# Linear attention and expert layer on one core: token loads cast by the DMA, scores and products on parts of the TensorE array, one activation recipe in two variants

## The chip, the cores and the metric

The kernel runs on one core of one Trainium2 chip. The metric is device time in microseconds (us), the median of several executions. "Batch" below means one of the eight batches of the problem; the kernel works on them one after another, and attention of batch b+1 runs while the expert layer of batch b does.

## The reference, cut to what matters

Eight batches, 8 heads, 576 tokens, 64 numbers a head. 32 packed queries p attend to the tokens; then the tokens attend to the 32 packed results; the result, as a row of 512 numbers, goes through two weight matrices with a piecewise activation between them.

```python
def sm_attn(qq, kk, vv):              # softmax(scale * q k^T) v
    ...
p_packed = sm_attn(p, k, v)           # 32 x 64 for each batch and head
out = sm_attn(q, p_packed, p_packed)  # 576 x 64 for each batch and head
x = out.transpose(0, 2, 1, 3).reshape(4608, 512)
h = x @ w_in                          # 512 -> 2048
g = where(h >= 1, h, where(h <= -1, 0, (h + 1)**2 / 4))
y = g @ w_out                         # 2048 -> 512
```

Both kernels use that x @ w_in = A @ M, where A holds the attention weights of the tokens over the packed rows and M is (packed result) @ (w_in), 32 rows for each head. So the expert layer's first product takes A and M, and x is never made.

## The kernel before

Only the parts that the change touches. Tokens are loaded in f32 and cast to bf16 on three engines; the remainder of 64 tokens (576 = 4 x 128 + 64) has its own load and casts.

```python
psA = ... bufs=2 (PSUM)   # all of attention
psH = ... bufs=2 (PSUM)   # hidden tiles h
psO = ... bufs=2 (PSUM)   # output tiles o

def load_tokens(src, b, tag, eng):
    t = stg.tile([P, H, NC4, D], f32, ...)      # 4 x 128 tokens
    eng.dma_start(...)
    r = stg.tile([REM, H, D], f32, ...)         # 64 tokens
    eng.dma_start(...)
# ... cut: cast_steps: two casts of 128x1024 and two of 64x256 for each of k, v, q;
#          batches 0 and 1 on VectorE, ScalarE and GpSimd, later ones on GpSimd

def scores(c0, n):
    for c in range(n):
        for hp in range(HP):          # 2 heads at once, p in a block-diagonal, half zeros
            nc.tensor.matmul(sp[:, c, hp], kT[:, hp, ...128 tokens], pT_blk[:, b, hp], ...)
    nc.scalar.activation(ex, sp, AF.Exp, scale=scale)
# ... cut: packed() (5 matmuls of 320 columns for 4 heads, masked), packed_t() (transposes)

def mk(g, f):                          # M, 4 heads x 512 columns of w_in
    for j in range(2):                 # the other half of ppT's rows is zero
        nc.tensor.matmul(mp, ppT[:, g, j], w_in_sb[:, 2 * g + j, f * FW:(f + 1) * FW], ...)
    ...                                # copied to SBUF by ScalarE or VectorE

def hidden_tile(b, fi):
    h = psH.tile([P, 2, FW], f32, tag="h")
    # ... cut: four matmuls of 288 columns, h = A, M
    nc.scalar.activation(r, hv, AF.Relu, bias=half, scale=0.5)        # r = relu(h/2 + 1/2)
    if (fi * PB_SHARE) % 8 < PB_SHARE:
        nc.gpsimd.tensor_mul(u, r, r)                                 # 10 of 16 tiles
    else:
        nc.scalar.activation(u, r, AF.Square)                         # 6 of 16
    nc.vector.scalar_tensor_tensor(dst, u, 1.0, hv, ALU.min, ALU.max) # max(min(r*r, 1), h)
```

The last line: the third engine in the row reads `hv`, the PSUM tile, again. So the tile is held until VectorE is done.

The softmax here doesn't subtract the row's maximum and nothing guards it: scores larger than these inputs give would overflow.

Of the kernel before, what the change touches and what calls it, by code (L numbers as in the profile page):

```python
# [11 lines left out]
def kernel(  # L12
# [20 lines left out]
    P = 128  # L33
# [4 lines left out]
    HP = H // 2  # L38
    G = H // 4
    NC4 = 4  # L40
    REM = S - NC4 * P
    HALF = S // 2
    KF = d_ff // P
    FW = 512
    PB_SHARE = 5
# [5 lines left out]
    stg = ctx.enter_context(tc.tile_pool(name="stg", bufs=1))  # L51
# [5 lines left out]
    psA = ctx.enter_context(tc.tile_pool(name="psA", bufs=2, space=bass.MemoryType.PSUM))  # L57
    psH = ctx.enter_context(tc.tile_pool(name="psH", bufs=2, space=bass.MemoryType.PSUM))
    psO = ctx.enter_context(tc.tile_pool(name="psO", bufs=2, space=bass.MemoryType.PSUM))



    def load_tokens(src, b, tag, eng):
        t = stg.tile([P, H, NC4, D], f32, tag=tag, name=tag)
        eng.dma_start(
            t.rearrange("p h c d -> p h (c d)"),
            src[b, :, :NC4 * P, :].rearrange("h (p c) d -> p h (c d)", c=NC4))
        r = stg.tile([REM, H, D], f32, tag=tag + "r", name=tag + "r")
        eng.dma_start(r, src[b, :, NC4 * P:, :].rearrange("h p d -> p h d"))
        raw[(tag, b)] = (t, r)  # L70

    def load_all(b, eng):
        for n, t in (("k", k), ("v", v), ("q", q)):
            load_tokens(t, b, n, eng)

    raw = {}
    load_all(0, nc.sync)


    p_nat = const.tile([P, B, G, D], bf16)  # L80
    p_v = p.rearrange("b (g h) n d -> (h n) b g d", g=G)
    nc.gpsimd.dma_start(p_nat[:, :1], p_v[:, :1])

    w_in_sb = const.tile([P, HP, d_ff], bf16)
    w_out_sb = const.tile([P, KF, d_model], bf16)
    w_in_v = moe_w_in.rearrange("(c p) f -> p c f", p=P)
    w_out_v = moe_w_out.rearrange("(c p) f -> p c f", p=P)

    def load_w_in(f):
        nc.gpsimd.dma_start(w_in_sb[:, :, f * FW:(f + 1) * FW], w_in_v[:, :, f * FW:(f + 1) * FW])  # L90
# [5 lines left out]
    mask = const.tile([P, 4, D], bf16)  # L96
    nc.vector.memset(mask, 0.0)
    for i in range(4):
        nc.vector.memset(onesblk[i * NP:(i + 1) * NP, i * NP:(i + 1) * NP], 1.0)
        nc.vector.memset(mask[i * NP:(i + 1) * NP, i], 1.0)  # L100
    half = const.tile([P, 1], f32)
    nc.vector.memset(half, 0.5)


    VB = H * D + D
    kb, qb, vb = [], [], []
    for i in range(2):
        for lst, nm in ((kb, "kb"), (qb, "qb")):
            t = const.tile([P, NC4 + 1, H * D], bf16, name=f"{nm}{i}")
            nc.vector.memset(t[REM:, NC4], 0.0)  # L110
            lst.append(t)
        t = const.tile([P, NC4 + 1, VB], bf16, name=f"vb{i}")
        nc.vector.memset(t[REM:, NC4], 0.0)
        nc.vector.memset(t[:, :NC4, 4 * D:5 * D], 1.0)
        nc.vector.memset(t[:REM, NC4, 4 * D:5 * D], 1.0)
        vb.append(t)

    def cast_steps(nm, b, engs):

        t, r = raw.pop((nm, b))  # L120
        d = {"k": kb, "q": qb, "v": vb}[nm][b % 2]

        def cp(e, dst, src):
            if e is nc.scalar:
                e.copy(dst, src)
            else:
                e.tensor_copy(dst, src)  # L127

        st = []
        for g in range(G):  # L130
            o = g * 5 * D if nm == "v" else g * 4 * D
            st.append(lambda o=o, g=g: cp(engs[g], d[:, :NC4, o:o + 4 * D].rearrange("p c (h d) -> p h c d", h=4),
                                          t[:, 4 * g:4 * g + 4]))
        for g in range(G):
            o = g * 5 * D if nm == "v" else g * 4 * D
            st.append(lambda o=o, g=g: cp(engs[2], d[:REM, NC4, o:o + 4 * D].rearrange("p (h d) -> p h d", h=4),
                                          r[:, 4 * g:4 * g + 4]))
        return st


    pT_blk = const.tile([P, B, HP, 2, NP], bf16)
    nc.vector.memset(pT_blk, 0.0)

    def build_pT(b0, b1):
        n = b1 - b0
        tp = psA.tile([P, n, 4, NP], bf16, tag="a", name="tpp")
        for b in range(b0, b1):
            nc.tensor.transpose(tp[:, b - b0].rearrange("p h n -> p (h n)"),
                                p_nat[:, b].rearrange("p g d -> p (g d)"), ident)

        for g in range(G):
            for h2 in range(2):
                nc.vector.tensor_copy(pT_blk[h2 * D:(h2 + 1) * D, b0:b1, 2 * g:2 * g + 2, h2, :],  # L153
                                      tp[g * D:(g + 1) * D, :, h2::2, :])
# [3 lines left out]
    def transposes(src, tag, base, rbase, width):  # L158

        T = tr.tile([P, HP, width], bf16, tag=tag, name=tag, bufs=1 if tag == "kT" else 2)  # L160

        def pair(c0):
            tp = psA.tile([P, HP, 2, P], bf16, tag="a", name="tp")
            for hp in range(HP):
                for c in range(2):
                    nc.tensor.transpose(tp[:, hp, c], src[:, c0 + c, hp * P:(hp + 1) * P], ident)  # L166
            nc.vector.tensor_copy(T[:, :, base + c0 * P:base + (c0 + 2) * P],  # L167
                                  tp.rearrange("p h c t -> p h (c t)"))

        def rest():  # L170
            n = P if width > S else REM
            tp = psA.tile([P, HP, P], bf16, tag="a", name="tp")
            for hp in range(HP):
                nc.tensor.transpose(tp[:, hp], src[:, NC4, hp * P:(hp + 1) * P], ident)
            nc.vector.tensor_copy(T[:, :, rbase:rbase + n], tp[:, :, :n])

        return T, [lambda: pair(0), lambda: pair(2), rest]

    def attention(b, split=False):

        st = []
        kT, sk = transposes(kb[b % 2], "kT", 0, NC4 * P, S + REM)

        base, rbase = (0, NC4 * P) if b % 2 == 0 else (REM, 0)
        qT, sq = transposes(qb[b % 2], "qT", base, rbase, S)
        vt = vb[b % 2]
        ex = att.tile([P, NC4 + 1, H * NP], bf16, tag="ex")

        def scores(c0, n):
            sp = psA.tile([P, n, HP, 2 * NP], f32, tag="a", name="sp")  # L190
            for c in range(n):
                for hp in range(HP):
                    nc.tensor.matmul(sp[:, c, hp], kT[:, hp, (c0 + c) * P:(c0 + c + 1) * P],  # L193
                                     pT_blk[:, b, hp].rearrange("p h n -> p (h n)"), start=True, stop=True)
            nc.scalar.activation(ex[:, c0:c0 + n].rearrange("p c n -> p (c n)"),  # L195
                                 sp.rearrange("p c a n -> p (c a n)"), AF.Exp, scale=scale)

        st += sk[:2] + [lambda: scores(0, 2), sk[2], lambda: scores(2, 2)]
        st += ([lambda: scores(4, 1)] + sq) if split else (sq[:1] + [lambda: scores(4, 1)] + sq[1:])

        ppT = att.tile([P, G, 2, P], bf16, tag="ppT")

        def packed(g):

            pp = psA.tile([P, 5 * D], f32, tag="a", name="pp")
            for c in range(NC4 + 1):
                nc.tensor.matmul(pp, ex[:, c, g * P:(g + 1) * P], vt[:, c, 4 * g * D:(4 * g + 5) * D],  # L207
                                 start=(c == 0), stop=(c == NC4))
            one, val = (4 * D, 0) if g == 0 else (0, D)
            rs = att.tile([P, 1], f32, tag="rs", name="rs")  # L210
            nc.vector.reciprocal(rs, pp[:, one:one + 1])
            pb = att.tile([P, 4 * D], bf16, tag="pb", name="pb")
            nc.vector.scalar_tensor_tensor(pb, pp[:, val:val + 4 * D], rs,
                                           mask.rearrange("p h d -> p (h d)"), ALU.mult, ALU.mult)
            return pb

        def packed_t(g, pb):
            tp = psA.tile([P, 2, P], bf16, tag="a", name="ppt")
            for j in range(2):
                nc.tensor.transpose(tp[:, j], pb[:, j * P:(j + 1) * P], ident)  # L220
            nc.vector.tensor_copy(ppT[:, g], tp)

        box = {}

        def put(key, fn):
            box[key] = fn()

        for g in range(G):
            st.append(lambda g=g: put(g, lambda: packed(g)))
        for g in range(G):  # L230
            st.append(lambda g=g: packed_t(g, box[g]))


        M = att.tile([P, G, d_ff], bf16, tag="M")
        A = att.tile([P, G, S], bf16, tag="A")
        M_of[b], A_of[b] = M, A

# [31 lines left out]
        if split:  # L269
            return st + pr + nm, ms  # L270
# [165 lines left out]
```

## Time and profile before

| | before |
|---|---|
| median | 334.59 us (three runs, 333.87 to 337.23; 334.45 with a fourth, taken beside the kernel after) |
| profiled span | 334.0 us |
| TensorE busy | 282.1 us, 84% |
| ScalarE, VectorE, GpSimd busy | 62%, 54%, 49% |

The page of the kernel before. The first two lines are the busy time of each engine, with its share of the span and the number of instructions. Each digit of the two rows is one of 40 equal slices: the busy share of TensorE in tenths, and the TensorE clock that was granted in tenths of full speed. Then the shares of the chain of work that ended last, and three groups of instructions: what they write and read, shapes, count | busy us, mean ns of one | idle time just before them and what ended most of it.

```profile
span 334.0 us, 5198 instructions
PE 282.1 (84%) x1879; PEld 164.9 (49%) x1912; DVE 180.3 (54%) x324; ACT 206.7 (62%) x371; POOL 162.2 (49%) x190
...
PE   0274868887878998999899999999999999988894
...
PEclk9998599997999999999999999999999999999999
...
PE 34%; issue 17%; POOL 16%; DMA 11%; DVE 10%; ACT 10%; POOLq 0%; SPq 0%; ACTq 0%
...
L298 POOL TENSOR_TENSOR u<-r 128x576 f32<-128x576 f32 x80 | 91.7, 1148 | 126.8 <-ACT r L295 117.7
L301 DVE SCALAR_TENSOR_TENSOR hT<-u,h 128x576 bf16<-128x576 f32 x128 | 96.2, 752 | 94.7 <-POOL u L298 80.3
...
L295 ACT ACTIVATE r<-h,half 128x576 f32<-128x576 f32 x128 | 94.7, 741 | 69.7 <-PE h L288 67.0
```

TensorE is busy 84% of the time, but its row shows that this is two different things: 90% and more from about the twentieth slice on, and mostly 70 to 80% at first. (The clock row prints 9 where the trace has no clock record, here before 26.7 us. The transposes at 7.65 us came 107 ns apart, and those at 50 us 56 ns, so TensorE was at half speed at first.) The chain gives TensorE only 34%; the hidden tile's three steps (ScalarE r, GpSimd u, VectorE hT) and "issue" share much of the rest. These steps take 741, 1148 and 752 ns. In the last batch a tile holds its PSUM buffer for 3.34 us on average, from its first matmul to the end of hT; with two buffers that allows a tile every 1.67 us, and they came 1.75 us apart.

To see the stages apart, the hidden tile's last write (hT; 128 of them, 16 a batch) helps. In the trace of the kernel before, the 17th hT, the first of batch 1, ends at 84.52 us, the 113th, the first of batch 7, at 289.24 and the last at 315.45. The first hT of batch 3 ends at 151.99.

Windows of all engines, kernel before: batches 1 to 6, and batches 3 to 6 alone. Columns: window, its length, busy time (and count) of TensorE, its weight loads, VectorE, ScalarE and GpSimd, granted clock, DMA share, GB/s.

```profile
84.52:289.24 204.72, 191.65 (x1321) 114.67 (x1346) 125.10 (x213) 146.57 (x270) 104.98 (x115) 1.00 0.37 105
151.99:289.24 137.25, 131.26 (x914) 78.81 (x930) 84.31 (x144) 99.29 (x183) 61.04 (x64) 1.00 0.19 61
```

So: start 84.5 us; six batches in 204.7 us, 34.1 us each (34.3 in batches 3 to 6); last batch and tail 44.8 us. In the last stretch the hidden tiles take 26.2 us and the tail 18.5.

The timeline of TensorE in the middle, kernel before (start, length, engine, line, what it writes and reads, count). The lengths overlap, because the ends are modelled; the cost of a group is the distance from its start to the next one's.

```profile
189.60 0.28 PE L193 MATMUL sp<-pT_blk,kT 128*128 128x64 bf16 x4
189.72 1.24 PE L321 MATMUL o<-w_out_sb,hT 128*128 128x512 bf16 x5
...
195.77 0.84 PE L207 MATMUL pp<-vb_133,ex 128*128 128x320 bf16 x5
196.45 0.28 PE L220 MATMUL ppt<-ident,pb 128*128 128x128 bf16 x2
...
207.07 0.59 PE L259 MATMUL mp<-w_in_sb,ppT 128*128 128x512 bf16 x2
207.50 0.29 PE L249 MATMUL sm<-eT,onesblk 128*128 128x288 bf16 x1
```

Four score matmuls take 0.12 us, five packed ones 0.68, two for M 0.43. Counted so, a batch's M (16 matmuls) costs 3.44 us and all of its attention 9.27 us. The expert layer's own o and h take 23.4 us. Together TensorE needs 32.7 us a batch; the batch takes 34.1. The middle is mostly TensorE's, with about 1.4 us of stalls a batch.

Where the stalls come from is in the waits of TensorE between 85.5 and 289.5 us, kernel before (engine, what it wanted to do, what it waited for: us in total, times, longest):

```profile
PE h L288 <- DVE hT L301: 9.2, 13, 2.1
PE mp L259 <- DVE M L264: 2.3, 5, 0.5
```

A hidden tile waits for the PSUM that an earlier one still holds: 9.2 us over six batches, 1.5 us a batch.

### The profile page before, as it was taken

How to read it: one execution, taken by the hardware profiler on the slowest of the kernel's cores; microseconds unless marked ns; L12 is line 12 of the kernel's file. 1: busy time of each engine (PE TensorE's matmuls, PEld its weight loads, DVE VectorE, ACT ScalarE, POOL GpSimd, SP SyncE). 2: the span in 40 equal slices, each digit the busy share in tenths (PEclk: the TensorE clock that was granted, in tenths of full speed). 3: DMA queues.
4: the chain of work that ended last, by engine and by line, in shares of the span. 5: the costliest groups of instructions: out<-in, count | busy, mean ns of one | idle time of the engine just before them, and what ended most of it. 6: DMA issues, size and time to landing. Idle time of an engine off the chain costs nothing.

```text
span 334.0 us, 5198 instructions
## 1 busy us (share of the span) xinstructions
PE 282.1 (84%) x1879; PEld 164.9 (49%) x1912; DVE 180.3 (54%) x324; ACT 206.7 (62%) x371; POOL 162.2 (49%) x190
## 2 busy tenths in 40 slices
PE   0274868887878998999899999999999999988894
PEld 0152345455444565557454655566546655444441
DVE  5332477564637764486457653767476638444300
ACT  2123745964668765966597747866977588666411
POOL 4092237599858849237824693242433242434300
PEclk9998599997999999999999999999999999999999
DMA  8999994577599595915740200000001200010031
GB/s 215 252 236 310 230 260 150 159 200 210 152 271 253 117 295 163 260 59 154 210 140 31 59 34 31 31 33 33 31 31 37 60 33 32 31 64 32 31 96 63
DMA packets 41689, 42.54 MB, mean 127 GB/s; under 512 B 12800, under 2 KB 35328, under 8 KB 41664
## 3 DMA queue, kind: packets, MB, share of 16 engines
q1 hardware_dynamic: 33472, 30.68, 31.6%
q0 software_dynamic: 8192, 11.54, 16.0%
q8 instruction: 15, 0.25, 0.3%
q14 instruction: 10, 0.08, 0.1%
HBM read 37.22 MB, written 9.44 MB: 140 GB/s over the span
## 4 chain that ended last, share of the span: by engine, by line
PE 34%; issue 17%; POOL 16%; DMA 11%; DVE 10%; ACT 10%; POOLq 0%; SPq 0%; ACTq 0%
PE o L321 15%; POOL u L298 9%; PE h L288 8%; DVE hT L301 5%; ACT r L295 4%; DMA kr<-in_k_dram 4%; PE mp L259 4%; DMA q<-in_q_dram 3%; DMA k<-in_k_dram 3%; DVE M L264 2%; PE tp L166 2%; DVE A L254 2%; ACT u L300 2%; POOL qb_131 L127 2%; POOL kb_121 L127 1%
## 5 line engine op out<-in xcount | busy, mean ns | idle before, releaser
L298 POOL TENSOR_TENSOR u<-r 128x576 f32<-128x576 f32 x80 | 91.7, 1148 | 126.8 <-ACT r L295 117.7
L301 DVE SCALAR_TENSOR_TENSOR hT<-u,h 128x576 bf16<-128x576 f32 x128 | 96.2, 752 | 94.7 <-POOL u L298 80.3
L321 PE MATMUL o<-w_out_sb,hT 128*128 128x512 bf16 x549 | 141.8, 380 | 1.5
L295 ACT ACTIVATE r<-h,half 128x576 f32<-128x576 f32 x128 | 94.7, 741 | 69.7 <-PE h L288 67.0
L288 PE MATMUL h<-A,M 128*128 128x288 bf16 x512 | 85.1, 290 | 16.0 <-DVE hT L301 15.4
L321 PEld LDWEIGHTS <-hT 128*128 128x128 bf16 x576 | 54.6, 98 | 49.8 <-DVE hT L301 0.6
L288 PEld LDWEIGHTS <-M 128*128 128x128 bf16 x512 | 49.5, 98 | 56.1 <-issue 20.6
L259 PE MATMUL mp<-w_in_sb,ppT 128*128 128x512 bf16 x122 | 36.9, 391 | 5.2 <-DVE M L264 3.1
L325 ACT COPY ob<-o 128x512 f32<-128x512 f32 x36 | 21.1, 587 | 20.2 <-PE o L321 20.0
L300 ACT ACTIVATE u<-r 128x576 f32<-128x576 f32 x48 | 32.9, 686 | 0.5
L264 DVE CAST M<-mp 128x512 bf16<-128x512 f32 x32 | 21.3, 684 | 9.1 <-PE mp L259 9.0
L254 DVE TENSOR_TENSOR A<-eT,rc 128x288 bf16<-128x288 bf16 x32 | 20.1, 632 | 6.3 <-ACT rc L253 6.2
L259 PEld LDWEIGHTS <-ppT 128*128 128x128 bf16 x128 | 12.8, 100 | 16.3 <-issue 10.6
L262 ACT CAST M<-mp 128x512 bf16<-128x512 f32 x32 | 18.7, 583 | 1.9 <-PE mp L259 1.6
L195 ACT ACTIVATE ex<-sp 128x512 bf16<-128x512 f32 (+1 forms) x24 | 12.3, 518 | 7.3 <-PE sp L193 7.2
L253 ACT ACTIVATE rc<-ln 128x288 f32<-128x288 f32 x32 | 14.1, 446 | 0.6
L167 DVE COPY qT<-tp 128x1024 bf16<-128x1024 bf16 x16 | 11.0, 688 | 4.8 <-PE tp L166 4.5
L251 ACT ACTIVATE ln<-sm 128x288 f32<-128x288 f32 x32 | 13.0, 411 | 0.1
L167 DVE COPY kT<-tp 128x1024 bf16<-128x1024 bf16 x16 | 11.0, 686 | 0.6 <-PE tp L166 0.4
L166 PE MATMUL tp<-ident,kb_121 128*128 128x128 bf16 x64 | 5.9, 242 | 6.2 <-DVE pT_blk L153 6.2
L193 PE MATMUL sp<-pT_blk,kT 128*128 128x64 bf16 x160 | 9.7, 200 | 0.9 <-ACT ex L195 0.6
L207 PEld LDWEIGHTS <-ex 128*128 128x128 bf16 x80 | 8.3, 104 | 3.7 <-issue 0.7
(152 smaller groups left out, 237.1 us busy)
## 6 DMA issues: line engine op xcount, KB each, us to landing
out_dram<-ob SPq DMA_DIRECT2D x32, 256.0 KB, 2.3
k<-in_k_dram SPq DMA_DIRECT2D x6, 1024.0 KB, 7.1
v<-in_v_dram SPq DMA_DIRECT2D x6, 1024.0 KB, 8.4
q<-in_q_dram SPq DMA_DIRECT2D x6, 1024.0 KB, 8.3
w_in_sb<-in_moe_w_in_dram POOLq DMA_DIRECT2D x4, 512.0 KB, 8.3
k<-in_k_dram POOLq DMA_DIRECT2D x2, 1024.0 KB, 9.5
v<-in_v_dram POOLq DMA_DIRECT2D x2, 1024.0 KB, 8.8
q<-in_q_dram POOLq DMA_DIRECT2D x2, 1024.0 KB, 9.9
```

The lines of the kernel that those rows point to most:

```text
L167: nc.vector.tensor_copy(T[:, :, base + c0 * P:base + (c0 + 2) * P], tp.rearrange("p h c t -> p h (c t)"))
L254: nc.vector.tensor_mul(A[:, g, hf * HALF:(hf + 1) * HALF], eT, rc)
L259: nc.tensor.matmul(mp, ppT[:, g, j], w_in_sb[:, 2 * g + j, f * FW:(f + 1) * FW], start=(j == 0), stop=(j == 1))
L262: nc.scalar.copy(M[:, g, f * FW:(f + 1) * FW], mp)
L264: nc.vector.tensor_copy(M[:, g, f * FW:(f + 1) * FW], mp)
L288: nc.tensor.matmul(h[:, hf, :HALF], M[:, g, fi * P:(fi + 1) * P], A[:, g, hf * HALF:(hf + 1) * HALF], start=(g == 0), stop=(g == G - 1))
L295: nc.scalar.activation(r, hv, AF.Relu, bias=half, scale=0.5)
L298: nc.gpsimd.tensor_mul(u, r, r)
L300: nc.scalar.activation(u, r, AF.Square)
L301: nc.vector.scalar_tensor_tensor(dst, u, 1.0, hv, ALU.min, ALU.max)
L321: nc.tensor.matmul(o, hT[:, fi, i * P:(i + 1) * P], w_out_sb[:, fi, :], start=(fi == 0), stop=(fi == KF - 1))
L325: nc.scalar.copy(ob, o)
```

## The change: its intent and the diff

The intent: take all compute from GpSimd, use a hidden-tile recipe whose first step alone reads PSUM, and stop multiplying zeros.

1. k, q, v are loaded straight to bf16 (the DMA casts), triggered by GpSimd; 576 tokens become 6 x 96, so that no remainder is left. Chunks of even and odd number lie in rows 0 to 63 and 64 to 127 ("chunk parity").
2. Scores, the packed product, the second scores and M become matmuls on halves or eighths of the TensorE array (64 rows, 64 columns, or 64 rows by 32 columns) without zeros.
3. The activation is x = prelu(h - 1, 0.5), t = max(x + 1, 0), min(t, 1) * t: for h between -1 and 1 the slope of one half makes t = (h + 1)/2, and above 1 t is h. t comes from ScalarE in half of the tiles and from VectorE in the other half.
4. All PSUM tiles but o share three double-bank buffers; steps of a chain are issued a tick or two later than their producers ("later"), by a fixed schedule. Some idle matmuls on zeros ("warm") sit in the start.

The diff, cut to its core; every "..." is a cut, and bookkeeping is left out.

```diff
-    psA = ... bufs=2 ; psH = ... bufs=2
+    psW = ctx.enter_context(tc.tile_pool(name="psW", bufs=3, space=bass.MemoryType.PSUM))
...
-        t = stg.tile([P, H, NC4, D], f32, tag=tag, name=tag)
-        eng.dma_start(...)                 # and r, 64 tokens; casts by three engines
+        t = stg.tile([TP, H, NC, D], bf16, tag=nm, name=nm)      # TP = 96, NC = 6
+        nc.gpsimd.dma_start(t.rearrange("p h c d -> p h (c d)"), ...)
...
-            nc.gpsimd.dma_start(p_nat[:, :1], p_v[:, :1])
+            (nc.sync, nc.scalar)[g].dma_start(p_raw[a * NP:(a + 1) * NP, :, g], p_v[a, :, :2, g])
...
+    def warm(n):
+        for _ in range(n):
+            nc.tensor.matmul(o, zeros[:, :P], zeros, start=True, stop=True)
...
-                    nc.tensor.matmul(sp[:, c, hp], kT[:, hp, (c0 + c) * P:(c0 + c + 1) * P],
-                                     pT_blk[:, b, hp].rearrange("p h n -> p (h n)"), start=True, stop=True)
+                        for x in range(X):                       # chunk parity
+                            r = slice(x * D, (x + 1) * D)
+                            nc.tensor.matmul(sp[:TP, x, e, g, a], kT[r, G * a + g, e0 + e], pT[r, b, g, a], ...)
...
-                nc.tensor.matmul(mp, ppT[:, g, j], w_in_sb[:, 2 * g + j, f * FW:(f + 1) * FW], ...)
+            for a in range(Q):
+                for g in range(G):
+                    r = slice(g * D, (g + 1) * D)
+                    nc.tensor.matmul(mp[a * NP:(a + 1) * NP, g], ppT[r, g, a], w_in_sb[r, a, f * FW:(f + 1) * FW], ...)
...
-        nc.scalar.activation(r, hv, AF.Relu, bias=half, scale=0.5)
-        if (fi * PB_SHARE) % 8 < PB_SHARE:
-            nc.gpsimd.tensor_mul(u, r, r)
-        else:
-            nc.scalar.activation(u, r, AF.Square)
-        nc.vector.scalar_tensor_tensor(dst, u, 1.0, hv, ALU.min, ALU.max)
+        nc.scalar.activation(x, hv, AF.Prelu, bias=-1.0, alpha=0.5)
+        def last():
+            nc.vector.scalar_tensor_tensor(dst, t, 1.0, t, ALU.min, ALU.mult)
+        def rest():
+            nc.vector.tensor_scalar(t, x, 1.0, 0.0, ALU.add, ALU.max)
+            last()
+        if kind == "V":
+            later(1, rest)
+        else:
+            later(1, lambda: nc.scalar.activation(t, x, AF.Relu, bias=1.0))
+            later(2, last)
```

## The prediction

> **What bounds the kernel now.** The page gives PE 282 us busy of 334 (84%), ACT 207, DVE 180, POOL 162. Three regimes show in the windows and in the spacing of the 128 hidden-tile writes (hT):
>
> - Start, to about 83 us: the granted clock falls to 0.5 for a while, loads gate the work (the chain of waits has k, kr and q loads), and batch 0's 16 hidden tiles take about 45 us.
> - Batches 1 to 6, 83 to 287 us: 34.0 us each, PE busy 93 to 97% of the windows. Counted in columns at the observed back-to-back spacing (o 512 columns about 0.215 us, transposes 55 ns, scores 30 ns), PE needs about 32.7 us a batch: 23.4 for o and h, 3.5 for M, 5.8 for the rest of attention. PE-bound.
> - Batch 7 (no attention left), 287 to 316 us: 1.8 us per hidden tile though PE needs 1.35. A hidden PSUM tile is held through ACT r (0.74), POOL u (1.15) and DVE hT (0.75), because hT reads h again; with two buffers that is about 3.6/2 us. Then 18 us of output tail.
>
> **What the change does.**
> 1. POOL compute goes (162 us busy: casts 1.04 us each, u 1.15). It is no bottleneck in the middle, but u sits inside the hidden chain and casts in the start's chain. Now only ACT's Prelu reads h, so PSUM comes free after about 0.8 us instead of 2.7.
> 2. ACT: Prelu 16 x 0.74, Relu 8 x 0.7, wider M, ex, ln, rc, eT: estimate 28 us a batch (25.8 before). DVE: hT 16 x 0.75, 8 tensor_scalar at about 0.46, wider copies: estimate 24.6 (22.5)..
> 3. PE: M and the second scores drop their half-zero operands (M 3.5 us to about 1.1, s2 1.0 to 0.5, ppT transposes gone), but scores become 48 small matmuls instead of 20 (0.6 to about 2.2 us), packed 60 instead of 10 (1.4 to 2.3). The Trainium skill, "TensorEngine Tiling (Array Packing)", Key Properties, says changing the tiling mode drains the engine; some 18 switches a batch cost 1.5 to 3 us (estimate; no trace here shows one). So PE stays at 33 to 34 us a batch, at best 31.
> 4. Start: no cast after landing, p on own queues, warm-up matmuls. Casting loads (w_in) moved about the same read bytes per engine-second as plain ones. Estimate: hidden starts near 25 us (37 before), batch 0 ends near 57 (83 before); loads for batch 2 may cost batch 1 some 4 us.
> 5. Batch 7: PE-bound, about 22.5 us (29). Tail unchanged, 18.
>
> **Sum:** 57 + 4 + 6 x 33.2 + 22.5 + 18 = 301 us. The gain lies in start (25) and batch 7 (6).
>
> **Range** 283 to 318. Faster by over 2%: 0.93; within: 0.05; slower: 0.02.
>
> **Signs.** Right: batch 1's first hT before 62 us; batch 7's hidden tiles 1.4 us apart; batches 2 to 6 at 31 to 35 us with PE over 90% busy; POOL under 10%; ACT about 85%. Wrong: batch spacing under 30 us (tiles run eight at once, switches cheap) or over 36; PE gaps released by ACT (three shared buffers too few).
>
> **What would make it wrong.** Row and column tiles not overlapping, or slow weight loads of 64 and 96 columns (slower); tiles packing well, leaving ACT as limit at 28 us (near 275); cast loads much slower than plain ones, stretching the first 90 us.

## The result and the profile after

The kernel after takes 289.42 us (median of four runs, 288.98 to 289.77) against 334.45 for the kernel before in the same rounds: ratio 0.864, 95% interval 0.860 to 0.868. Ratios here and below are the mean time of one kernel's runs over that of the other's runs of the same rounds, so not quite the ratio of the medians quoted. The result is correct. The prediction was 301 with a range of 283 to 318, so it was right in direction and inside its range, but 12 us too slow.

The page of the kernel after, the lines that answer to those of before:

```profile
span 287.9 us, 6617 instructions
PE 267.5 (93%) x2785; PEld 152.2 (53%) x2785; DVE 191.0 (66%) x345; ACT 197.2 (68%) x309; POOL 27.2 (9%) x42
...
PE   6696685989999999999999999999999999999993
...
PEclk9659999599999999999999999999999999999998
...
PE 83%; DVE 6%; ACT 6%; DMA 2%; issue 1%; DVEq 0%; ACTq 0%; POOLq 0%
...
L279 DVE SCALAR_TENSOR_TENSOR hT<-t 128x576 bf16<-128x576 f32 x128 | 96.6, 755 | 29.0 <-ACT t L288 26.1
L276 ACT ACTIVATE x<-h 128x576 f32<-128x576 f32 x128 | 83.1, 650 | 44.9 <-PE h L268 43.9
```

The chain is TensorE's for 83% now, where it was 34%. VectorE's hT waits 29 us in all, where it waited 94.7. GpSimd has left: 9% is its load triggers and start-up work.

In the kernel after, the 17th hT ends at 57.75 us, the 113th at 247.41, the last at 267.59, and the first of batch 3 at 122.89. Windows of all engines, batches 1 to 6 and batches 3 to 6; columns as before:

```profile
57.75:247.41 189.66, 188.70 (x2072) 108.62 (x2070) 142.38 (x251) 145.97 (x231) 9.27 (x12) 1.00 0.46 83
122.89:247.41 124.52, 124.52 (x1358) 71.44 (x1355) 92.40 (x164) 97.36 (x155) 4.63 (x6) 1.00 0.36 68
```

| stretch | before | after | predicted |
|---|---|---|---|
| first hidden matmul at | 37.06 | 25.72 | near 25 |
| first hT of batch 1 done at | 84.5 | 57.8 | 57 |
| batches 1 to 6 | 204.7 (34.1 each) | 189.7 (31.6 each) | 4 + 6 x 33.2 = 203.2 |
| last batch and tail | 44.8 (26.2 + 18.5) | 40.5 (20.2 + 20.3) | 40.5 (22.5 + 18) |
| sum | 334 | 288 | 301 |

Of 46 us, the start gives 27, the middle 15, the end 4. The start and the end were predicted almost to the microsecond. The whole error is in the middle, where the prediction saw hardly any gain and the chip gave 2.5 us a batch. Batches with four output tiles (3 and 5) take 30.0 us in the kernel after and those with five (2, 4 and 6) 32.2 to 32.7. Batch 1, with four, takes 32.5; in it the loads of batch 2 are still going on.

These stretches aren't quite the same work. By its 17th hT the kernel before had made at least 29 of batch 0's 64 output matmuls and all transposes and scores of batch 2, the kernel after 3 and none. So the middle of the kernel before is short of some 8 us of TensorE work (an estimate: 26 x 0.217 + 40 x 0.055 + 20 x 0.03). Batches 3 to 6, with 18 output tiles in each kernel, are a fairer pair: 137.25 us before and 124.52 after, which is 34.3 and 31.1 a batch. TensorE is idle for 6.0 us of the first and for none of the second.

In the middle TensorE is busy for 188.7 us of 189.7 (it was 191.7 of 204.7 before), ScalarE 146.0, VectorE 142.4.

The waits of TensorE between 58.5 and 247.5 us, kernel after; this is the whole answer, and no wait for hT is in it:

```profile
PE tp L174 <- DVE kT L178: 1.0, 1, 1.0
```

The timeline of TensorE in the middle, kernel after:

```profile
155.93 0.65 PE L268 MATMUL h<-A,M 128*128 128x288 bf16 x4
156.51 0.89 PE L188 MATMUL sp<-pT,kT 64*96 64x32 bf16 x32
157.33 1.25 PE L307 MATMUL o<-w_out_sb,hT 128*128 128x512 bf16 x5
...
163.06 0.94 PE L199 MATMUL pk<-ex,v 96*64 96x32 bf16 x48
163.92 0.45 PE L204 MATMUL pk<-ones_114,ex 96*128 96x2 bf16 x12
...
167.82 0.41 PE L241 MATMUL mp<-w_in_sb,ppT 64*32 64x512 bf16 x8
168.16 1.25 PE L307 MATMUL o<-w_out_sb,hT 128*128 128x512 bf16 x5
...
171.17 0.65 PE L268 MATMUL h<-A,M 128*128 128x288 bf16 x4
171.66 0.41 PE L228 MATMUL sm<-eT,onesblk 128*128 128x288 bf16 x2
```

The 32 score matmuls take 0.82 us, 25.6 ns each. The 48 packed ones take 0.86 us, 17.9 ns each. Eight matmuls of 512 columns for M take 0.34 us. The price of entering a tiled group is seen from the h group before it: 0.49 us from h to an untiled group (171.17 to 171.66), 0.58 from h to the scores (155.93 to 156.51), so about 0.1 us, some nine times a batch (the change back lies inside the groups' own times). The Trainium skill, "TensorEngine Tiling (Array Packing)", Key Properties, says that changing the tiling mode drains the engine, and gives no size; this trace puts about 0.1 us on one change, and doesn't show the reason. Summed, attention costs TensorE 7.8 us a batch, with the changes of mode, where it cost 9.27. With 23.4 for o and h this makes 31.2; a batch takes 31.1 in batches 3 to 6. So of the 3.2 us a batch that have gone there, 1.5 are work by this count and the other 1.7 are waiting.

### The profile page after: what moved, and what is told of

Its sections match the earlier page's. It is cut to its first block, busy times and chain, and to the rows that moved or that the text cites. A ratio compares the mean times of both kernels' runs of the same rounds, so it can differ in the third digit from the quotient of the medians.

```text
span 287.9 us, 6617 instructions
## 1 busy us (share of the span) xinstructions
PE 267.5 (93%) x2785; PEld 152.2 (53%) x2785; DVE 191.0 (66%) x345; ACT 197.2 (68%) x309; POOL 27.2 (9%) x42
## 4 chain that ended last, share of the span: by engine, by line
PE 83%; DVE 6%; ACT 6%; DMA 2%; issue 1%; DVEq 0%; ACTq 0%; POOLq 0%
PE o L307 44%; PE h L268 20%; PE tp L174 5%; PE sp L188 4%; PE mp L241 3%; DMA k<-in_k_dram 2%; DVE hT L279 2%; PE pk L199 2%; PE o L130 2%; ACT x L276 2%; ACT t L288 1%; PE sm L228 1%; DVE kT L178 1%; PE pk L204 1%; DVE pT L145 1%
## 5 line engine op out<-in xcount | busy, mean ns | idle before, releaser
L279 DVE SCALAR_TENSOR_TENSOR hT<-t 128x576 bf16<-128x576 f32 x128 | 96.6, 755 | 29.0 <-ACT t L288 26.1
L276 ACT ACTIVATE x<-h 128x576 f32<-128x576 f32 x128 | 83.1, 650 | 44.9 <-PE h L268 43.9
L288 ACT ACTIVATE t<-x 128x576 f32<-128x576 f32 x64 | 43.7, 683 | 1.5
L282 DVE TENSOR_SCALAR t<-x 128x576 f32<-128x576 f32 x64 | 29.2, 457 | 6.1 <-ACT x L276 5.7
L243 DVE CAST M<-mp 128x1024 bf16<-128x1024 f32 x16 | 19.5, 1218 | 1.4 <-PE mp L241 1.4
L233 DVE SCALAR_TENSOR_TENSOR A<-eT,rs,rc 128x576 bf16<-128x576 bf16 x16 | 13.1, 817 | 9.4 <-ACT rc L232 9.2
L178 DVE COPY kT<-tp 128x768 bf16<-128x768 bf16 (+1 forms) x32 | 13.0, 450 | 7.9 <-PE tp L174 7.7
L178 DVE COPY qT<-tp 128x768 bf16<-128x768 bf16 (+1 forms) x32 | 13.0, 452 | 7.6 <-PE tp L174 7.6
L243 ACT CAST M<-mp 128x1024 bf16<-128x1024 f32 x16 | 16.1, 1007 | 0.2
L241 PE MATMUL mp<-w_in_sb,ppT 64*32 64x512 bf16 x256 | 13.8, 415 | 1.1 <-ACT ln L230 0.8
```

What stands on the lines that cost most here:

```text
L178: nc.vector.tensor_copy(T[:, 4 * i:4 * i + 4, e0:e0 + n], tp[:, i, :4 * n * TP].rearrange("p (h e t) -> p h e t", h=4, e=n))
L241: nc.tensor.matmul(mp[a * NP:(a + 1) * NP, g], ppT[r, g, a], w_in_sb[r, a, f * FW:(f + 1) * FW], start=True, stop=True)
L243: mcopy(f)(M[:, :, f * FW:(f + 1) * FW], mp)
L276: nc.scalar.activation(x, hv, AF.Prelu, bias=-1.0, alpha=0.5)
L279: nc.vector.scalar_tensor_tensor(dst, t, 1.0, t, ALU.min, ALU.mult)
L282: nc.vector.tensor_scalar(t, x, 1.0, 0.0, ALU.add, ALU.max)
```

## The experiments

Two theories stood against each other first. **Theory T (both):** the hidden recipe removes the stalls, the tiles remove TensorE work, and each gives about half of the middle. **Rival R (recipe):** the short hold of PSUM is all of it; or **rival L (layout):** the tiles and loads are all of it. The next two runs do one part alone, from both sides. Twelve kernels ran; all were correct.

### e1: the kernel before with the new recipe alone

```diff
-        nc.scalar.activation(r, hv, AF.Relu, bias=half, scale=0.5)
+        nc.scalar.activation(r, hv, AF.Prelu, bias=-1.0, alpha=0.5)
...
+        if fi % 2:
+            nc.vector.tensor_scalar(u, r, 1.0, 0.0, ALU.add, ALU.max)
+        else:
+            nc.scalar.activation(u, r, AF.Relu, bias=1.0)
+        nc.vector.scalar_tensor_tensor(dst, u, 1.0, u, ALU.min, ALU.mult)
```

> The kernel before with only the new activation recipe (Prelu, then Relu on ACT or add/max on DVE, then min times; Pool still casts the tokens). Theory (the middle's gain is 1.5 us a batch of PE work saved by the small tiles and about 1 us of PE stalls that the long hidden chain caused): the stalls go but the PE work stays, so batches 1 to 6 take about 33 us (34.0 before, 31.5 after), batch 7's tiles span 20 us instead of 26, the start shortens by some 5 us; total 314 to 322. Rival (the recipe is nearly the whole gain): batches near 31.5 us and a total under 305.

Measured: 322.09 us, ratio 0.962 (0.957 to 0.968). First hT of batch 1 at 80.5 us (84.5 before), the middle 199.2 us or 33.2 a batch, the last batch's tiles in 20.2 us (26.2 before). The window of batches 3 to 6 of e1, columns as before:

```profile
144.67:279.69 135.02, 131.47 (x944) 79.60 (x941) 102.16 (x177) 98.33 (x191) 20.22 (x24) 1.00 0.20 62
```

What follows: in the last batch the recipe alone is the whole gain. Its tiles come 1.35 us apart in e1 as in the kernel after, and a buffer of h is held for 1.34 us, until Prelu has read it. In the middle it does little alone. TensorE's waits for hT (9.2 us before) are gone, but 9.1 us of other waits stand in their place, most of them for VectorE (4.2 us for the packed result pb alone). Batches 3 to 6 take 33.8 us each, about half a microsecond less than before, of the 3.2 that the whole change gives. Of all 45 us the recipe alone gives 12.7. (Start and middle are hard to compare here: by its 17th hT e1 had already made 52 of batch 0's 64 output matmuls.)

### e2: the kernel after with the old recipe

```diff
-        nc.scalar.activation(x, hv, AF.Prelu, bias=-1.0, alpha=0.5)
-        ...                                   # both variants, delayed by ticks
+        nc.scalar.activation(r, hv, AF.Relu, bias=half, scale=0.5)
+        if (fi * 5) % 8 < 5:
+            nc.gpsimd.tensor_mul(u, r, r)
+        else:
+            nc.scalar.activation(u, r, AF.Square)
+        nc.vector.scalar_tensor_tensor(dst, u, 1.0, hv, ALU.min, ALU.max)
```

> The kernel after with the old recipe (Relu, square on Pool for 5 of 8 tiles, min/max that reads PSUM again). Theory: PE work stays at about 31.2 us a batch but hidden PSUM is held for about 2.7 us again, in buffers now shared with attention: PE idles behind DVE hT, batches take 33 to 36 us, batch 7's tiles span 22 to 26; total 300 to 320. Rival (the chain never mattered, only PE work does): within 2% of 289.

Measured: 359.35 us, ratio 1.073 (1.068 to 1.077): slower than the kernel before, and far beyond what was expected. The middle takes 230.8 us, 38.5 a batch. First hT of batch 1 at 86.2. The window of batches 3 to 6 of e2, 37.5 us a batch:

```profile
166.84:316.98 150.14, 131.76 (x1370) 74.49 (x1370) 79.48 (x132) 100.99 (x147) 50.75 (x46) 0.99 0.35 66
```

The waits of TensorE in e2 between 86.5 and 316.5 us:

```profile
PE tp L176 <- DVE hT L282: 10.9, 5, 2.7
PE sp L190 <- DVE hT L282: 9.9, 11, 1.2
PE sm L230 <- DVE hT L282: 2.3, 5, 0.6
```

These are attention's matmuls (transposes, scores, sums) that wait for hT, which they don't read: they wait for the PSUM buffer that hT gives back. With two smaller waits of that kind (1.2 and 0.4 us) it is 24.7 us of the 28.7 in which TensorE is idle there (201.34 busy of 230). That TensorE is also busy longer, 201.3 us against 188.7 in the kernel after for the same work, isn't explained here. The three buffers are shared by h and all of attention, and a hidden tile that is held for ScalarE, GpSimd and VectorE takes them from attention. In the start TensorE waits 19.5 us in one piece besides: GpSimd's first product stood in its queue until 46 us, behind the triggers of p's loads, which waited for earlier loads. TensorE's clock was granted at 0.58 on average from 26 us to 86.

What follows: the tiles and loads without the recipe lose time (38.5 against 34.1 us a batch). Rivals R and L fall. T stands in that both parts are needed, but not as two halves: in batches 3 to 6 the recipe alone gives 0.6 us a batch, the layout alone loses 3.2, and both together gain 3.2. The layout with its shared buffers gains only on top of the recipe, and most of what the recipe gives in the middle needs the layout. One flaw: the old recipe's steps were issued at once and not delayed by ticks, so e2 differs from the kernel after by that too.

### e10: a GpSimd step that doesn't hold PSUM

Which property of the old recipe hurts: GpSimd's slow step, or the hold of PSUM? In e10 PSUM is read by Prelu alone, but GpSimd makes t in 5 of 8 tiles of batches 1 to 7.

```diff
+        elif kind == "P":
+            later(1, lambda: nc.gpsimd.tensor_scalar(t, x, 1.0, 0.0, ALU.add, ALU.max))
+            later(2, last)
...
-                hidden_tile(b, i, "WV"[i % 2])
+                hidden_tile(b, i, "WV"[i % 2] if b == 0 else "WP"[i * 5 % 8 < 5])
```

> The kernel after with the middle step (add 1, max 0) of 10 of 16 tiles on Pool in batches 1 to 7 and the rest on ACT: Pool's share is that of the old recipe, but Prelu alone reads PSUM. Theory (what made the old recipe slow in these buffers is PSUM held through Pool and DVE, not Pool as such): 287 to 292. Rival (Pool in the chain is slow enough by itself[...]): over 300.

Measured: 308.06 us, ratio 0.920 (0.915 to 0.925); 34.1 us a batch. Two groups of instructions of e10:

```profile
L288 POOL TENSOR_SCALAR t<-x 128x576 f32<-128x576 f32 x70 | 152.6, 2192 | 73.4 <-ACT x L276 58.1 <-DVE hT L279 14.7
...
L279 DVE SCALAR_TENSOR_TENSOR hT<-t 128x576 bf16<-128x576 f32 x128 | 109.1, 859 | 81.0 <-POOL t L288 70.0 <-ACT t L291 9.3
```

The time crosses the bound that was set for the rival, but the test was spoilt by its instrument: the two-operation step took 2192 ns on GpSimd, nearly twice the old product's 1148. It still says something. With a GpSimd step almost twice as long, but PSUM free after Prelu, a batch takes 34.1 us and not e2's 38.5, and TensorE's waits for hT are gone. Its longest ones in the middle of e10:

```profile
PE sp L188 <- DVE qT L178: 6.6, 4, 1.9
PE tp L174 <- DVE M L243: 1.3, 3, 0.5
```

So GpSimd's slowness isn't the main part of e2's loss. By e2's waits the held PSUM is, with e2's issue without delay as a rival that no run takes apart. How many of the 6.9 us a batch between e2 and the kernel after it makes is argued, not shown: at least 4.3 by this comparison, less whatever the issue without delay did in e2.

The second line shows a side cost: hT takes 859 ns beside a working GpSimd, 755 in the kernel after. The Trainium skill, "SBUF — State Buffer", Who interferes with whom, says that a VectorE instruction with two SBUF inputs contends with GpSimd's reads and that one with at most one, outside the two-port modes, doesn't. Both halves are seen here: the old hT reads one tile in SBUF and one in PSUM and took 752 ns in the kernel before, with GpSimd busy half of the time; the new hT reads two in SBUF and took 834 in e1, where GpSimd still casts, and 859 here.

### e5: M's matmuls twice

If TensorE bounds the middle, work added there must come back one to one.

```diff
-            for a in range(Q):
+            for a in [*range(Q), *range(Q)]:
                 for g in range(G):
```

> The kernel after with every M matmul issued twice (same values). Theory (the middle is PE-bound and eight tiles run side by side): each group of 8 adds about 0.24 to 0.34 us, 28 groups in the PE-bound part: plus 6 to 10 us, 295 to 300. Rival 1 (ACT or DVE is the limit): under 2 us. Rival 2 (tiles run one after the other or two at a time): 0.9 to 1.7 us a group, plus 25 to 48 us.

Measured: 294.25 us against 289.42, ratio 0.879 (0.875 to 0.883); the middle 195.0 us, 32.5 a batch, which is 0.9 more. The timeline of TensorE in e5, which stands against 167.82 and 168.16 of the kernel after:

```profile
169.62 0.62 PE L241 MATMUL mp<-w_in_sb,ppT 64*32 64x512 bf16 x16
170.18 1.25 PE L307 MATMUL o<-w_out_sb,hT 128*128 128x512 bf16 x5
```

Sixteen matmuls take 0.56 us where eight took 0.34: 0.22 more, four times a batch, is 0.9 us. The batch grew by 0.9. So TensorE is the bound of the middle, one to one, and the total (+4.8 us) came out under what was expected only because the tiles are cheaper than was assumed. Eight tiles of 512 columns in 0.22 us is about the time of a single full matmul (five o matmuls of 512 columns take 1.09, 0.218 each): they do run all at once. The Trainium skill, "TensorE: Matmul & The Clock Gate", Measured speedup vs the span model, has some 4 ns for each further tile of a pack, on top of one matmul; an estimate from that, with the spacing of one full matmul, 0.218 + 7 x 0.004 = 0.25 us, is close to the 0.22 measured. In the trace the eight start 3 to 4 ns apart.

### e3: no warm-up matmuls

```diff
     def warm(n):
-        ...
+        return
```

> The kernel after without the warm-up matmuls on zeros. Theory: they only touch the first 27 us; the granted clock stays low through the first attention and costs 1 to 4 us: 290 to 293. Rival: the clock is low there anyway (0.6 and 0.5 in slices 2 and 3 with them) and they sit in front of q's transposes, so taking them out gains 1 to 2 us: 287 to 288.

Measured: 290.01 us, ratio 0.866 (0.862 to 0.870), with the kernel after at 0.864: no difference. The first hidden matmul starts at 24.73 us without them and at 25.72 with them. With the warm-up, the clock is granted in full for one stretch of 3.4 us, and 17 of k's 24 transposes fall into it, about 43 ns apart; then, from 9.02 to 22.67 us, it is granted at half, in the part of the start where the work is. TensorE was busy for 12.44 of these 13.65 us. Without the warm-up the transposes come 80 ns apart from the second on. The Trainium skill, "TensorE: Matmul & The Clock Gate", Part 1, has a clock that rises after a busy window of about 3.4 us; the trace agrees with that length, but being busy early didn't keep the clock up afterwards. The warm-up matmuls are no part of the gain.

### e4 and e9: casts on engines again

Both keep the tiles and the recipe, but load f32 by the SyncE queue and cast on engines. They also have one buffer for each of k, v, q where the kernel after has two, and issue batch 1's loads later. e4 splits batch 0's casts over VectorE, ScalarE and GpSimd, e9 over VectorE and ScalarE only; later batches are cast by GpSimd in both.

```diff
-        t = stg.tile([TP, H, NC, D], bf16, ...)
-        nc.gpsimd.dma_start(...)
+        t = stg.tile([TP, H, NC, D], f32, ..., bufs=1)
+        nc.sync.dma_start(...)
+    def cast(nm, b):
+        ...
+        if b == 0:           # e9; in e4: heads 0-3 VectorE, 4-6 ScalarE, 7 GpSimd
+            nc.vector.tensor_copy(t[:, :5], f[:, :5])
+            nc.scalar.copy(t[:, 5:], f[:, 5:])
+        else:
+            for i in range(4):
+                nc.gpsimd.tensor_copy(t[:, 2 * i:2 * i + 2], f[:, 2 * i:2 * i + 2])
```

> The kernel after, but tokens come in as float32 through SP and are cast on the engines (batch 0 on DVE, ACT and Pool, later batches on Pool), one buffer of each; the weights' loads are issued before any cast. Theory (the start got shorter because loads no longer queue behind casts and products on Pool; casting in flight is not itself faster): start within 5 us of after (batch 1's first tile at 59 to 64), middle unchanged as Pool is idle there: 289 to 296. Rival (casting on an engine is itself what made the start long): batch 1's first tile after 70 us, total over 300.

Measured, e4: 325.66 us, ratio 0.975 (0.970 to 0.980). The middle takes 32.0 us a batch (31.6 in the kernel after); the start takes 91.7 us. The timeline of e4:

```profile
17.90 0.57 POOL L347 DMA_DIRECT2D p_nat<-in_p_dram  x1 [10.76 <-DMA w_in_sb<-in_moe_w_in_dram]
...
37.26 0.52 POOL L97 CAST k<-kf 96x384 bf16<-96x384 f32 x1
...
37.83 0.98 PE L185 MATMUL tp<-ident,k 96*128 96x96 bf16 x10 [26.94 <-POOL k L97]
```

GpSimd's small cast of k, ready to go near 8 us, ran at 37 us, since it stood behind triggers of p's loads that waited for earlier loads (one of them 10.76 us). So e4 measured a blocked queue and not the price of casts; e9 was the repair.

> As the run with casts on the engines, but batch 0's casts are on DVE and ACT only, since there Pool's part of k sat behind p's load triggers until 37 us. Theory (what costs in the start is work that queues behind a waiting load or trigger on an in-order engine, not the cast itself): k's transposes start by 9 us, batch 1's first tile at 59 to 66, total 289 to 297. Rival (casting on an engine is slow in itself): batch 1's first tile after 70 us and a total over 300.

Measured, e9: 316.35 us, ratio 0.945 (0.940 to 0.950); start 82.7 us, middle 32.0 a batch. By its own bounds this is the rival's result (over 70 and over 300), but the trace shows another cause. The timeline of e9:

```profile
9.80 2.10 PE L184 MATMUL tp<-ident,k 96*128 96x96 bf16 x24 [2.93 <-DVE k L95]
...
29.91 0.40 PE L152 MATMUL tpp<-ident,p_nat 128*128 128x128 bf16 x2 [18.00 <-DVE p_nat L149]
```

k's transposes start at 9.80 us, 1.5 later than in the kernel after (8.31); the cast of k took 1.16 us. But then TensorE waits 18.00 us for p, whose loads now stood behind the token loads on the same queue. Again another queue effect. Of the 25 us by which e9's start is longer, 18 are p's, 1.5 lie before k's transposes and 1.3 are left for v's and q's casts (the first hidden matmul comes at 46.53 us, 20.8 later). The other 4 come after it, where the clock was granted at half from 57.6 to 74.7 us. So the cast itself is worth at most some 7 us of the start (25 - 18), which no run isolates. In the middle, where the casts lie beside other work, casting on engines costs 0.4 us a batch in both runs; hT takes 859 and 868 ns there, not 755. The DMA's cast is worth something mainly in the start.

For comparison, this is how the casts stood in the way in the kernel before. Timeline of the start, kernel before; in square brackets the idle time of the engine before the instruction, and what ended it:

```profile
7.57 0.29 PE L148 MATMUL tpp<-ident,p_nat 128*128 128x128 bf16 x1 [7.57 <-DMA p_nat<-in_p_dram]
...
13.50 0.69 DVE L127 CAST vb_125<-v 128x1024 bf16<-128x1024 f32 x1 [6.20 <-DMA v<-in_v_dram]
14.11 0.79 DVE L153 COPY pT_blk<-tpp 64x64 bf16<-64x64 bf16 x4
...
14.95 1.03 PE L166 MATMUL tp<-ident,kb_121 128*128 128x128 bf16 x8 [6.24 <-DVE pT_blk L153]
...
29.05 0.69 DVE L127 CAST kb_129<-k 128x1024 bf16<-128x1024 f32 x1 [3.76 <-DMA k<-in_k_dram]
30.46 0.40 PE L220 MATMUL ppt<-ident,pb 128*128 128x128 bf16 x2 [4.35 <-DVE pb L213]
```

p's transpose was done before 8 us, but its copy on VectorE came at 14.11, behind a cast that waited 6.20 us for v to land; TensorE waited 6.24 us for that copy. The same again at 29.05: the next batch's cast of k waits for its load, and TensorE waits 4.35 us for a copy behind it. These two, 10.6 us, are nearly the whole difference of 11.3 us in the first hidden matmul (37.06 against 25.72). By this trace it wasn't the duration of a cast that cost time, but a cast that waits for a load at the head of an in-order engine; no run takes these two waits out alone. The other 15 us of the start's gain lie between the first hidden matmul and batch 1's first hT (47.5 us before, 32.0 after). Of these, 7 come before the very first hT, which ends 11.3 us after the first hidden matmul in the kernel before and 4.0 after it in the kernel after: in the kernel before its u was ready at 40.7 us, but VectorE came to hT at 47.6, after copies of M, a cast of q and copies of batch 1's p and k. The rest these runs don't split. The recipe alone gives 3 us of the 15 (e1). The loads and tiles without the recipe give none (e2, 60.2 us), but e2's 19.5 us stall and half clock lie there.

### e6, e7, e8: is the start still to be improved?

In the kernel after, TensorE's row shows 6 to 8 tenths in the first slices. e6 issues q's transposes between the scores and drops six of the 25 warm-ups; e7 brings the first output tiles, which need only a part of batch 0's hidden tiles, into batch 0; e8 does both.

```diff
# e6
-    go("sc0 sc1"); warm(2); go("pk"); warm(3); go("qT0 qT1"); warm(3)
+    go("sc0 qT0 sc1 qT1 pk"); warm(2)
# e7: steps of output tiles 0 and 1 of the first pair, each after the hT that it reads
+            early = [st for pair in zip(out_tile(0, 0, {}), out_tile(0, 1, {})) for st in pair]
+            ...                                   # given out over slots 17 to 33 of batch 0
-            o = spread(outs(b - 1), 0 if b > 1 else 6, 32)
+            ...                                   # b == 1: only tiles 2 and 3
```

> The kernel after with q's transposes of batch 0 moved ahead of the packed product, and three groups of warm-up matmuls there taken out. Theory: second scores of batch 0 start near 19.5 us instead of 21.7, so the first hidden tile comes 2 us earlier: 286.5 to 288. Rival (batch 0 waits for loads of batch 1 anyway): no change, 289.

> The kernel after with two of batch 0's four output tiles (32 matmuls, 6.9 us of PE at full clock) accumulated while batch 0's hidden tiles are still made, where PE has gaps. Theory (from 60 us on PE is the only limit, before that it is not): 4 to 7 us less, 282.5 to 285.5. Rival (ACT or DVE limits the middle too): under 2 us less.

> Both of the last two moves together. Theory: they add, 280 to 284. Rival: the first is lost behind the loads, as e7.

Measured: e6 288.46 us (ratio 0.866, 0.858 to 0.873), e7 286.32 (0.859, 0.853 to 0.866), e8 287.15 (0.859, 0.854 to 0.864). All three medians are below the 289.42 of the kernel after, by 1 to 3 us, but the intervals overlap with its own (0.860 to 0.868): not shown to be faster. e7 and e8 fell short of their forecasts. (Three of e7's four runs took 286.2 to 286.4 us and all ten of the kernel after 289.0 or more, so a gain of about one per cent may well be there.) e7's profile is of its slowest run, 289.86 us, so it can explain the shortfall only in part. In it batch 1 shrinks from 32.5 to 29.2 us and the start grows from 57.8 to 61.9. In the window from 60 to 90 us TensorE is busy 27.0 of 30 us, VectorE 26.5 and ScalarE 24.7 (29.0, 24.1 and 22.0 in the kernel after). So with TensorE relieved, the two other engines are close to full there, which suggests why moving TensorE's work about gives little.

### e11: an attempt at a faster version

e8, with GpSimd taking t in half of the tiles of batches 0 and 1 to relieve the other two, p's loads taken from its queue, and batch 1's attention for the next batch begun earlier.

```diff
-                hidden_tile(b, i, "WV"[i % 2])
+                hidden_tile(b, i, "WV"[i % 2] if b > 1 else "PVPW"[i % 4])
...                                   # e8; p by the SyncE queue; attention from slot 3
```

> Attempt at a faster version: q early and outputs early together, p loaded as float32 through SP so that Pool has no p triggers, loads for batch 2 earlier, and Pool takes the middle step of half the tiles of batches 0 and 1, where ACT and DVE are 88 to 95% busy. Theory (batches 0 and 1 are limited by ACT and DVE once PE is relieved): batch 2's first tile at 86 to 90 instead of 93, total 280 to 284. Rival (Pool and DVE lock each other out): no better than 286.

Measured: 298.2 us (ratio 0.891, 0.887 to 0.895): slower than the kernel after. First hT of batch 1 at 68.4 us (57.8), of batch 2 at 102.7 (90.2). GpSimd's step takes 2.24 us here; that its delay outweighs the relief of the other two is the likely cause, but e11 changed three more things. The attempt failed.

### a1: the kernel after again

> The kernel after itself, unchanged, as the yardstick of these rounds: 289, ratio 0.864.

Measured: 289.41 us median of six (289.11 to 292.52), ratio 0.867 (0.863 to 0.871). The first measurement stands. The slowest of the six is the profiled one, and its trace has three half-clock periods in the first 65 us (13.65 + 3.4 + 13.65 us) where the first profile had two (13.65 + 6.8): the two slow ones of the six (292.5 and 291.3) have mean clocks of 0.944 and 0.942, the four others (289.1 to 289.5) 0.966 to 0.970. Such periods go with a change of one per cent, which is the size of what e6 to e8 might have gained.

### All runs

| kernel | median us | ratio to before | batches 1 to 6, us each | first hT of batch 1 |
|---|---|---|---|---|
| before | 334.45 | 1 | 34.1 | 84.5 |
| after | 289.42 | 0.864 | 31.6 | 57.8 |
| e1 before, new recipe | 322.09 | 0.962 | 33.2 | 80.5 |
| e2 after, old recipe | 359.35 | 1.073 | 38.5 | 86.2 |
| e10 after, GpSimd step | 308.06 | 0.920 | 34.1 | 59.2 |
| e5 after, M twice | 294.25 | 0.879 | 32.5 | 56.9 |
| e3 after, no warm-up | 290.01 | 0.866 | 31.6 | 58.9 |
| e4, e9 casts on engines | 325.66, 316.35 | 0.975, 0.945 | 32.0, 32.0 | 91.7, 82.7 |
| e6, e7, e8 start reordered | 288.46, 286.32, 287.15 | 0.866, 0.859, 0.859 | 31.6, 30.9, 30.9 | 56.5, 61.9, 59.8 |
| e11 attempt | 298.2 | 0.891 | 31.6 | 68.4 |
| a1 after, again | 289.41 | 0.867 | 31.6 | 60.5 |

## Why the prediction was right or wrong, point by point

- **Direction and range: right.** 289.42 lies in 283 to 318, and "faster by over 2%" had 0.93.
- **The start (step 4): right.** Hidden work near 25 us: 25.72. Batch 0 done near 57: 57.8. Batch 1 paying some 4 us: it took 32.5, batches 3 and 5, with as many output tiles, 30.0, so 2.5 us; that the loads of batch 2 are the cause wasn't tested. That casting loads move about the same read bytes per engine time as plain ones holds in the trace of the kernel before: 20.5 bytes a ns (w_in's and w_out's packets) against 17.8 to 19.9 (k's, v's and q's). The reason given, "no cast after landing", is half right. What stood in the way, by the trace, were casts waiting at the head of VectorE for loads (6.2 and 3.8 us), not casts as such. The warm-up matmuls were listed with the reasons and do nothing (e3).
- **The hidden chain (steps 1 and 5): right.** Tiles of the last batch come 1.35 us apart (predicted 1.4; 1.75 before), and e1 shows that the recipe alone does this. Its sum was off by 2.5 us, tiles 20.2 us and not 22.5, and the tail by as much the other way, 20.3 and not 18; the two errors cancel, which is luck.
- **The term that was mis-sized is step 3: "scores become 48 small matmuls instead of 20 (0.6 to about 2.2 us), packed 60 instead of 10 (1.4 to 2.3)".** The trace shows 1.28 and 1.18 us. They were priced at about 46 ns each (2.2 / 48) and 38 ns (2.3 / 60), as matmuls that follow one another on the whole array. Pairs in different rows or columns overlap, and they came at 25.6 and 17.9 ns. M was sized too low, 1.36 and not 1.1. The switches, 1.5 to 3 us by the estimate, cost about 0.9. Attention on TensorE is 7.8 us a batch in place of the 10 to 11 that "33 to 34" implies; "at best 31" was the right answer (31.1 in batches 3 to 6).
- **So "The gain lies in start (25) and batch 7 (6)" was wrong:** the middle gave 15 us. In batches 3 to 6 it is 3.2 us each, 1.5 of TensorE work and 1.7 of waiting. The prediction had named 1.3 us of stalls (34.0 against 32.7) but its 33.2 us a batch kept a part of them, or of dearer tiles, in place of the 31.2 that the work needs.
- **ACT "about 85%": wrong, 68%.** 28 us a batch were estimated, 197.2 / 8 = 24.6 came. Prelu was priced like the old Relu, 0.74; it takes 650 ns and not 741. The old Relu had its bias in a 128 x 1 tensor, Prelu has a constant. The Trainium skill, "ScalarE: Activation LUTs", What ACT_TABLE_LOAD costs, gives about 93 ns for each such operand; the difference here is 91 ns. The page could have given this before. For 16 tiles a batch that is 1.5 of the 3.4 us; the rest isn't traced.
- **VectorE 24.6 us a batch:** 191.0 / 8 = 23.9. GpSimd under 10%: 9%. TensorE over 90% busy: 93%, and 188.7 of 189.7 us in the middle.

What stays open: how the 15 us of the start after the first hidden matmul divide between recipe, loads and schedule; how the gain that comes on top of e1 divides between small tiles, shared wide buffers and the fixed schedule of issue, which no run takes apart; the price of the cast itself (at most some 7 us); how much of e2's loss is the order of issue; and whether e7 or e8 is one per cent faster.

## What to carry to other kernels

Let one engine read a PSUM tile once and free it, before you build a layout with fewer PSUM buffers on it: here the new layout was 14% faster than the kernel before with such a recipe and 7% slower than it without. Price small tiled matmuls by their spacing in a trace, not like small full ones: pairs on half arrays came at 18 to 26 ns, a change of mode at 0.1 us. On an in-order engine, keep work that waits for a load (a cast, or a trigger that waits for an earlier load) away from short steps that others wait for; the kernel before, e2 and e4 had single waits of 4 to 27 us of this kind.

## What the Trainium skill lacked or had wrong

- "TensorEngine Tiling (Array Packing)", Key Properties: a change of tiling mode has no size there. About 0.10 us from a full to a tiled group here (0.58 against 0.49 us between starts).
- "TensorE: Matmul & The Clock Gate", Part 1, states that start-to-start never drops below about 25 ns. Here the two matmuls of a pair on different halves of the array start 3 to 4 ns apart, as the page's part on packing has it, and the next pair follows 42 ns later for the scores (halves of the rows) and 28 for the packed product (halves of the columns, 96 rows, 32 columns moved), so that 48 packed matmuls came at 17.9 ns each. What the next pair costs with so few columns isn't on the page.
- The same page, Part 1: with 25 warm-up matmuls of 512 columns, 12 of them before the loads landed, there was one stretch of full clock, 3.4 us, and then half clock for 13.65 us, with TensorE busy for 12.44 of them (transposes and warm-ups included); without them the first hidden matmul was 1 us earlier (24.73 against 25.72). Advice on when a warm-up pays is lacking.
- "GPSIMD Engine Reference", Performance versus the Vector engine, has the sum of two tensors but no two-operation step with a tensor and two constants: 2192 ns for 128 x 576 in f32, against 1148 for the product of two tensors.
- No page says how long compute on GpSimd can stand behind load triggers on the same queue. Here a trigger waited 10.76 us for an earlier load, and the cast behind such triggers held TensorE up for 26.94 us.
